# A gated recurrence followed by a highway layer: loads in runs of 4 KB, a product transposed by plain matmuls, and three products in two PSUM slots

## The chip, the cores and the metric

The kernel runs on one core of a Trainium2 chip. The metric is the device time of one execution in microseconds; lower is better. Times of a kernel are given as the median of its runs, with the lowest and highest.

## What is computed

The input has 4 sequences of 6336 tokens with 256 channels. First a gated linear recurrence runs along each sequence, for every channel on its own; then a highway layer with two 256 x 256 weights is applied to every token of the result. Cut to what matters:

```python
sig = 1.0 / (1.0 + np.exp(-f_logit))
f = lower_bound + (1.0 - lower_bound) * sig
i = 1.0 - f
for t in range(S):
    h = f[:, t] * h + i[:, t] * x[:, t]
    y[:, t] = h
...
H = np.maximum(y @ w_h, 0.0)
T = 1.0 / (1.0 + np.exp(-(y @ w_t + b_t)))
out = T * H + (1.0 - T) * y
```

Inputs and output are float32. x, f_logit and the output have 26 MB each, so about 78 MB cross the memory interface.

## The kernel before

**Tiling.** The tokens are cut into 29 units of work. Two small ones hold the first 192 tokens of two sequences each, on 96 partitions. The rest goes in steps of 1024 tokens, sequence by sequence, so that the four recurrences are carried side by side: a unit has 8 blocks of 128 tokens. The first such unit is split in two of 512 tokens, the last in 512, 256 and 256. There are 22 full units. The 256 channels are handled as two halves of 128.

**One unit, step by step.**

- `load` (L76) brings `lt` (from f_logit) and `xt` (from x) into SBUF, tokens on partitions. A partition gets one token of each block, so each run in memory is one token, 1 KB. Loads and stores are issued on SP's queue, four units ahead.
- `gate` (L140), on ACT, makes `u = sigmoid(-lt)` in float16. `product` (L152), on GpSimd (POOL), makes `bv = u * xt` in bfloat16.
- `decay_pe` (L178) and `b_pe` (L192) transpose `u` and `bv` on TensorE (PE) into PSUM (`uT`, `bT`), with channels on partitions and time along the row. Each transposes blocks of 128 x 128, eight for a half unit.
- `decay_act` (L185), on ACT, makes the decay `f = 1 + (lb - 1) u` from `uT`.
- `scan` (L201), on VectorE (DVE), runs the recurrence over `f` and `bT` into `y`; a half unit is one instruction of 1024 steps.
- `g_pe` and `z_pe` (both through `ffn_pe`, L212) multiply `y` by the weights, into PSUM tiles `gp` and `zp`.
- `t_act` (L227), on ACT, makes `t = sigmoid(z + b)` from `zp`. `d_dve` (L233), on DVE, makes `d` from `gp` and `y`; `e_dve` (L242) makes `e = d * t`, three quarters on DVE and one quarter on GpSimd.
- `o_pe` (L257) brings `y` and `e` back to tokens on partitions, with 16 matmuls for each half of four blocks, into PSUM tile `op`; the stationary operand takes every fourth column, so that a partition holds four tokens that follow each other. `o_act` (L271) copies `op` to SBUF on ACT and stores it in runs of 4 KB.

For units of 512 tokens and fewer, `both` (L164) puts the two channel halves into one PSUM tile.

**Order.** The order on each engine is written out by hand in the loop from L282 and pinned, so that PE, DVE, ACT and POOL take their instructions in just that order. With `n` the unit that is scanned, `p = n - 1` and `pp = n - 2`, one turn of the loop gives, for full units:

```
PE:  z(p,0)  o(pp,0)  uT(n+1,0)  bT(n,1)  z(p,1)  g(p,1)  o(pp,1)  bT(n+1,0)  uT(n+1,1)  g(n,0)
ACT: t(p,0)  o copy(pp,0)  f(n+1,0)  t(p,1)  u(n+2)  o copy(pp,1)  f(n+1,1)
DVE: scan(n,0)  d(p,0)  scan(n,1)  d(p,1)  e(p)
```

**PSUM.** A PSUM tile is taken from a pool by its tag, and a slot is given out again when the last reader of its former tile is done. The eight banks of 2 KB per partition are used thus, all from the pool `ps1` with one slot for each tag:

| tile | type, size per partition | slots |
|---|---|---|
| uT | float16, 2 KB | 1 |
| bT | bfloat16, 2 KB | 1 |
| gp | float32, 4 KB | 1 |
| zp | float32, 4 KB | 1 |
| op | float32, 4 KB | 1 |

Of the kernel before, what the change touches and what calls it, by code (L numbers as in the profile page):

```python
# [11 lines left out]
FP32 = mybir.dt.float32  # L12
BF16 = mybir.dt.bfloat16
FP16 = mybir.dt.float16
AF = mybir.ActivationFunctionType
# [4 lines left out]
def kernel(  # L20
# [16 lines left out]
    nc = tc.nc  # L37
    B, S, D = x.shape
    assert D == 256
    P = 128  # L40
    NH = D // P
    NB = 8
# [5 lines left out]
    units = []  # L48
# [4 lines left out]
    for s0 in range(rest, S, NB * P):  # L53
        for b in range(B):
            last = s0 + NB * P == S and b == B - 1
            a = s0
# [11 lines left out]
    outp = ctx.enter_context(tc.tile_pool(name="outp", bufs=4))  # L68
    ps1 = ctx.enter_context(tc.tile_pool(name="ps1", bufs=1, space=bass.MemoryType.PSUM))

    st = [dict() for _ in range(NU)]

    def pin(ins):
        return tc.keep_in_program_order(ins)

    def load(n, name, src):  # L76
        np_, nb, _, b, a = units[n]
        t = inp.tile([P, NB, D], FP32, tag=name, name=name)
        if isinstance(b, int):
            pin(nc.sync.dma_start(t[:, :nb], src[b, a:a + nb * P, :].rearrange("(j p) d -> p j d", p=P)))  # L80
        else:
            t4 = t[:np_, :nb].rearrange("p (b j) d -> p b j d", j=2)
            for j in range(2):
                pin(nc.sync.dma_start(t4[:, :, j], src[b, a + j * np_:a + (j + 1) * np_, :].rearrange("b p d -> p b d")))
        st[n][name] = t

    def store(n, j0, j1):
# [19 lines left out]
    for n in range(2):  # L107
        load(n, "lt", f_logit)
        load(n, "xt", x)

    ident_b = singles.tile([P, P], BF16, name="ident_b")
# [6 lines left out]
    ncc = singles.tile([P, NH], FP32, name="ncc")  # L118
# [42 lines left out]
    def width(n):  # L161
        return units[n][0] * units[n][1]

    def both(n, m, key, make):  # L164


        if width(n) > 512:
            st[n][key, m] = make()
            yield st[n][key, m], m, 0
        elif m == 0:  # L170
            st[n][key, 0] = st[n][key, 1] = t = make()
            for k in range(NH):
                yield t, k, k * 512

    def col(n, m):
        return 0 if width(n) > 512 else m * 512

    def decay_pe(n, m):  # L178
        np_, nb = units[n][:2]
        for uT, h, c in both(n, m, "uT", lambda: ps1.tile([P, NB * P], FP16, tag="uT", name="uT")):  # L180
            for j in range(nb):
                pin(nc.tensor.transpose(uT[:, c + j * np_:c + (j + 1) * np_], st[n]["u"][:np_, j, h * P:(h + 1) * P],  # L182
                                        ident_h[:np_, :np_]))

    def decay_act(n, h):  # L185
        N, c = width(n), col(n, h)
        if h == 0:
            st[n]["f"] = mid.tile([P, NH, NB * P], FP16, tag="f", name="f")
        pin(nc.scalar.activation(st[n]["f"][:, h, :N], st[n]["uT", h][:, c:c + N], AF.Identity,  # L189
                                 scale=ncc[:, h:h + 1], bias=1.0))  # L190

    def b_pe(n, m):  # L192
        np_, nb = units[n][:2]
        for bT, h, c in both(n, m, "bT", lambda: ps1.tile([P, NB * P], BF16, tag="bT", name="bT")):
            for j in range(nb):
                pin(nc.tensor.transpose(bT[:, c + j * np_:c + (j + 1) * np_], st[n]["bv"][:np_, j, h * P:(h + 1) * P],  # L196
                                        ident_b[:np_, :np_]))

    carry = {}

# [10 lines left out]

    def ffn_pe(n, m, key, k):  # L212
        N = width(n)
        for p, h, c in both(n, m, key, lambda: ps1.tile([P, NB * P], FP32, tag=key, name=key)):
            for ki in range(NH):
                for a in range(0, N, 512):
                    e = min(a + 512, N)
                    pin(nc.tensor.matmul(p[:, c + a:c + e], w_sb[:, k, ki, h * P:(h + 1) * P], st[n]["y"][:, ki, a:e],  # L218
                                         start=ki == 0, stop=ki == NH - 1))

    def g_pe(n, m):
        ffn_pe(n, m, "gp", 0)

    def z_pe(n, m):
        ffn_pe(n, m, "zp", 1)
# [29 lines left out]
    QB = NB // 2  # L255

    def o_pe(n, q):  # L257
        op = ps1.tile([P, QB, D], FP32, tag="op")
        np_, nb, _, b, _ = units[n]
        j0, j1 = q * QB, min((q + 1) * QB, nb)  # L260
        g = j1 - j0 if isinstance(b, int) else 2
        for j in range(j0, j1):
            k, i = divmod(j - j0, g)
            cols = slice((j0 + k * g) * np_ + i, (j0 + (k + 1) * g) * np_, g)
            for h in range(NH):
                o = op[:np_, j - j0, h * P:(h + 1) * P]
                pin(nc.tensor.matmul(o, st[n]["y"][:, h, cols], diag[:, h], start=True, stop=False))  # L267
                pin(nc.tensor.matmul(o, st[n]["e"][:, h, cols], ident_b, start=False, stop=True))  # L268
        st[n]["op"] = op
# [12 lines left out]
    for n in range(-3, NU + 2):  # L282
        if ok(n + 4) and n + 4 > 1:
            load(n + 4, "lt", f_logit)
            load(n + 4, "xt", x)
        p, pp = n - 1, n - 2
# [8 lines left out]
        if ok(pp):  # L295
            o_pe(pp, 0)
            o_act(pp, 0)
        if ok(n + 1):
            decay_pe(n + 1, 0)
            decay_act(n + 1, 0)  # L300
        if ok(p):
            d_dve(p, 0)
        if ok(n):
            b_pe(n, 1)
# [14 lines left out]
        if ok(pp) and units[pp][1] > QB:  # L319
            o_pe(pp, 1)  # L320
            o_act(pp, 1)
        if ok(n + 1):
            b_pe(n + 1, 0)
            decay_pe(n + 1, 1)
            decay_act(n + 1, 1)
# [38 lines left out]
```

## Time and profile before

Two runs took 228.53 and 225.68 us; the median is 227.11 us. The profiled execution has a span of 226.9 us from the first to the last instruction; the page gives no other time of its own for that execution.

| engine | busy us | share of the span |
|---|---|---|
| PE (matmul) | 195.0 | 86% |
| DVE | 202.1 | 89% |
| ACT | 199.1 | 88% |
| POOL | 140.0 | 62% |

The main groups on the engines, full units alone:

| line | operation | count | mean ns |
|---|---|---|---|
| L207 | DVE scan, 1024 steps | 44 | 2342 |
| L237 | DVE d, 1024 elements | 44 | 1256 |
| L249 | DVE e, 1536 elements | 22 | 958 |
| L143 | ACT u, 2048 elements | 22 | 1927 |
| L189 | ACT f, 1024 elements | 44 | 1136 |
| L231 | ACT t, 1024 elements | 44 | 1119 |
| L276 | ACT copy of o, 1024 elements | 47 | 1013 |
| L156 | POOL product, 512 elements | 96 | 1171 |

The DMA moved 78.69 MB in 60262 packets, 53584 of them under 2 KB, at a mean of 347 GB/s.

How to read it: busy time counts an engine from the start to the end of its instructions, and matmuls overlap each other in the records, so that PE's share says little about how close PE is to its limit; the distance between the starts of matmuls says more. A share over the whole span also mixes the start, the steady part and the tail. The steady part is read from a table by stage and from a timeline, and what counts there is the distance from one unit's scan to the next unit's. The row PEclk gives the clock that TensorE was granted, in tenths of full speed.

### The profile page before, as it was taken

The page shows a single profiled execution, that of the slowest core. Times are in us where ns is not written, and L with a number is a line of the kernel's source. Part 1 is how long each engine was busy: PE and PEld are TensorE (multiplying, and loading weights), DVE is VectorE, ACT ScalarE, POOL GpSimd, SP SyncE. Part 2 cuts the span into 40 slices and gives each one's busy share as a digit, 9 for nine tenths or more (in the row PEclk, how much of TensorE's full clock was granted, in tenths as well). Part 3 has the DMA queues.
Part 4 walks back from the last instruction along what each step waited for, and adds up shares of the span by engine and source line. Part 5 has one row for each costly group of instructions (what it writes and reads, how often), then busy time and mean ns, then how long its engine had stood idle before and what let it go on. Part 6 is the DMA issues. An engine that isn't in the chain of part 4 may idle for free.

```text
span 226.9 us, 4999 instructions
## 1 busy us (share of the span) xinstructions
PE 195.0 (86%) x2008; PEld 136.9 (60%) x2008; DVE 202.1 (89%) x159; ACT 199.1 (88%) x198; POOL 140.0 (62%) x131
## 2 busy tenths in 40 slices
PE   0588495989999999999999999999999999998971
PEld 0356365656766666676666657666665766665661
DVE  1499657799999999999999999999999999999871
ACT  4459946799999999999999999999999999976873
POOL 2654870745966786696678669667866966764300
PEclk9999857899999999999999999999999999999998
DMA  6999999999999999999999999999999997542444
GB/s 179 307 386 386 383 390 390 390 390 387 399 385 385 399 394 389 384 397 382 382 391 395 388 390 402 395 384 403 396 387 397 396 349 276 202 185 95 185 185 185
DMA packets 60262, 78.69 MB, mean 347 GB/s; under 512 B 2384, under 2 KB 53584, under 8 KB 60240
## 3 DMA queue, kind: packets, MB, share of 16 engines
q1 hardware_dynamic: 59152, 77.86, 93.9%
q10 hardware_dynamic: 1088, 0.53, 0.9%
q8 instruction: 15, 0.25, 0.4%
q14 instruction: 7, 0.06, 0.1%
HBM read 52.43 MB, written 25.95 MB: 345 GB/s over the span
## 4 chain that ended last, share of the span: by engine, by line
DVE 52%; issue 23%; PE 13%; DMA 4%; ACT 3%; POOL 3%; DVEq 0%; SPq 0%; ACTq 0%; POOLq 0%
DVE y L207 25%; DVE d L237 19%; DVE e L249 8%; PE gp L218 4%; PE zp L218 3%; POOL bv L156 3%; DMA xt<-in_x_dram 2%; PE bT L196 2%; PE uT L182 2%; DMA lt<-in_f_logit_dram 1%; PE op L267 1%; PE op L268 1%; ACT o L276 1%; ACT u L143 1%; ACT t L231 1%
## 5 line engine op out<-in xcount | busy, mean ns | idle before, releaser
L156 POOL TENSOR_TENSOR bv<-u,xt 128x512 bf16<-128x512 f16 (+1 forms) x100 | 114.3, 1172 | 18.9 <-DMA xt<-in_x_dram 7.2
L207 DVE TENSOR_TENSOR_SCAN y<-f,y,bT 128x1024 bf16<-128x1024 f16 (+2 forms) x54 | 113.7, 2105 | 7.9 <-PE bT L196 7.6
L231 ACT ACTIVATE t<-zp,bt 128x1024 bf16<-128x1024 f32 (+3 forms) x58 | 56.9, 994 | 13.5 <-PE zp L218 13.5
L218 PEld LDWEIGHTS <-w_sb 128*128 128x128 f16 x408 | 39.7, 100 | 43.1 <-issue 10.0
L237 DVE SCALAR_TENSOR_TENSOR d<-y,ncc,gp 128x1024 bf16<-128x1024 bf16 (+3 forms) x58 | 63.8, 1101 | 1.0 <-PE gp L218 0.9
L189 ACT ACTIVATE f<-uT,ncc 128x1024 f16<-128x1024 f16 (+3 forms) x58 | 58.4, 1007 | 4.2 <-PE uT L182 4.2
L251 POOL TENSOR_TENSOR e<-d,t 128x512 bf16<-128x512 bf16 x22 | 25.5, 1159 | 56.3 <-PE gp L218 56.3
L218 PE MATMUL gp<-y,w_sb 128*128 128x512 bf16 (+2 forms) x204 | 53.3, 385 | 3.7 <-DVE d L237 1.3
L218 PE MATMUL zp<-y,w_sb 128*128 128x512 bf16 (+2 forms) x204 | 52.6, 382 | 0.1
L267 PE MATMUL op<-diag,y 128*128 128x128 f16 (+1 forms) x400 | 50.8, 221 | 2.2 <-ACT o L276 2.2
L276 ACT COPY o<-op 128x1024 f32<-128x1024 f32 (+2 forms) x51 | 50.9, 997 | 1.9 <-PE op L268 1.7
L143 ACT ACTIVATE u<-lt 128x2048 f16<-128x2048 f32 (+3 forms) x29 | 49.0, 1689 | 3.9 <-DMA lt<-in_f_logit_dram 3.9
L268 PE MATMUL op<-ident_b,e 128*128 128x128 bf16 (+1 forms) x400 | 50.8, 220 | 0.0
L268 PEld LDWEIGHTS <-e 128*128 128x128 bf16 (+1 forms) x400 | 44.9, 115 | 7.5 <-POOL bv L156 1.3
L267 PEld LDWEIGHTS <-y 128*128 128x128 bf16 (+1 forms) x400 | 45.0, 114 | 5.7 <-issue 0.3
L196 PE MATMUL bT<-ident_b,bv 128*128 128x128 bf16 (+1 forms) x400 | 32.8, 224 | 16.6 <-DVE y L207 8.3
L196 PEld LDWEIGHTS <-bv 128*128 128x128 bf16 (+1 forms) x400 | 26.9, 100 | 23.8 <-issue 15.2
L182 PE MATMUL uT<-ident_h,u 128*128 128x128 f16 (+1 forms) x400 | 32.4, 227 | 5.7 <-ACT u L143 5.7
L182 PEld LDWEIGHTS <-u 128*128 128x128 f16 (+1 forms) x400 | 26.1, 103 | 6.1 <-ACT u L143 5.7
L249 DVE TENSOR_TENSOR e<-d,t 128x1536 bf16<-128x1536 bf16 (+3 forms) x29 | 25.9, 892 | 3.6 <-ACT t L231 0.8
L207 DVE TENSOR_TENSOR_SCAN y<-f,bT 128x192 bf16<-128x192 f16 x8 | 3.9, 536 | 4.1 <-PE bT L196 4.1
L117 DVE TENSOR_SCALAR cc<-lb 128x2 f32<-128x2 f32 x1 | 0.2, 169 | 3.8 <-DMA lb<-in_lower_bound_dram 3.8
(16 smaller groups left out, 6.8 us busy)
## 6 DMA issues: line engine op xcount, KB each, us to landing
out_dram<-o SPq DMA_DIRECT2D x47, 512.0 KB, 7.2
lt<-in_f_logit_dram SPq DMA_DIRECT2D x22, 1024.0 KB, 9.4
xt<-in_x_dram SPq DMA_DIRECT2D x22, 1024.0 KB, 11.3
lt<-in_f_logit_dram SPq DMA_DIRECT2D x3, 512.0 KB, 7.6
xt<-in_x_dram SPq DMA_DIRECT2D x3, 512.0 KB, 6.7
lt<-in_f_logit_dram SPq DMA_DIRECT2D x4, 192.0 KB, 3.7
xt<-in_x_dram SPq DMA_DIRECT2D x4, 192.0 KB, 3.9
out_dram<-o SPq DMA_DIRECT2D x2, 384.0 KB, 9.3
```

Of the source, the lines that this page charges most:

```text
L143: pin(nc.scalar.activation(u[:np_, :nb], st[n]["lt"][:np_, :nb], AF.Sigmoid, scale=-1.0))
L156: ins = pin(nc.gpsimd.tensor_mul(bv[:np_, q:q + 2], st[n]["u"][:np_, q:q + 2], st[n]["xt"][:np_, q:q + 2]))
L182: pin(nc.tensor.transpose(uT[:, c + j * np_:c + (j + 1) * np_], st[n]["u"][:np_, j, h * P:(h + 1) * P], ident_h[:np_, :np_]))
L189: pin(nc.scalar.activation(st[n]["f"][:, h, :N], st[n]["uT", h][:, c:c + N], AF.Identity, scale=ncc[:, h:h + 1], bias=1.0))
L196: pin(nc.tensor.transpose(bT[:, c + j * np_:c + (j + 1) * np_], st[n]["bv"][:np_, j, h * P:(h + 1) * P], ident_b[:np_, :np_]))
L207: pin(nc.vector.tensor_tensor_scan(y[:, h, c0:c0 + ln], st[n]["f"][:, h, c0:c0 + ln], st[n]["bT", h][:, col(n, h) + c0:col(n, h) + c0 + ln ...
L218: pin(nc.tensor.matmul(p[:, c + a:c + e], w_sb[:, k, ki, h * P:(h + 1) * P], st[n]["y"][:, ki, a:e], start=ki == 0, stop=ki == NH - 1))
L231: pin(nc.scalar.activation(st[n]["t"][:, m, :N], st[n]["zp", m][:, c:c + N], AF.Sigmoid, bias=bt[:, m:m + 1]))
L237: pin(nc.vector.scalar_tensor_tensor(st[n]["d"][:, m, :N], st[n]["y"][:, m, :N], ncc[:, m:m + 1], st[n]["gp", m][:, c:c + N], op0=ALU.mult ...
L267: pin(nc.tensor.matmul(o, st[n]["y"][:, h, cols], diag[:, h], start=True, stop=False))
L268: pin(nc.tensor.matmul(o, st[n]["e"][:, h, cols], ident_b, start=False, stop=True))
L276: pin(nc.scalar.copy(st[n]["o"][:np_, j0:j1], st[n]["op"][:np_, :j1 - j0]))
```

## The change

Three things are changed together.

1. **Loads.** A partition now gets four tokens that follow each other (for the small first units and the units of 256 tokens two), so that a run is 4 KB (or 2 KB). The first two units' loads are one transfer each in place of two. Blocks therefore hold every fourth token, and the columns have to be brought into time order on the way to the scan.
2. **Time order.** For `f`, ACT reads `uT` at a step and writes in time order. For `bT`, PE writes at a step: the transposes become plain matmuls with the identity, whose output is float32 at a step of four words (two for the small units). `bT` so grows from 2 KB to 4 KB per partition.
3. **PSUM.** `uT` moves to a pool with two slots. `gp`, `zp` and `op` share one tag, `zg`, with two slots of 4 KB. The sum is again eight banks: 4 KB for `bT`, 2 x 4 KB for `zg`, 2 x 2 KB for `uT`.

`o_pe` computes its columns with the same step as before (four, and two for the small units). The loop and its order on each engine are not touched.

```diff
+    ps2 = ctx.enter_context(tc.tile_pool(name="ps2", bufs=2, space=bass.MemoryType.PSUM))
+
+    ps3 = ctx.enter_context(tc.tile_pool(name="ps3", bufs=2, space=bass.MemoryType.PSUM))
...
         if isinstance(b, int):
-            pin(nc.sync.dma_start(t[:, :nb], src[b, a:a + nb * P, :].rearrange("(j p) d -> p j d", p=P)))
+            g = min(nb, 4)
+            pin(nc.sync.dma_start(t[:, :nb].rearrange("p (s j) d -> p s j d", j=g),
+                                  src[b, a:a + nb * P, :].rearrange("(s p j) d -> p s j d", p=P, j=g)))
         else:
-            t4 = t[:np_, :nb].rearrange("p (b j) d -> p b j d", j=2)
-            for j in range(2):
-                pin(nc.sync.dma_start(t4[:, :, j], src[b, a + j * np_:a + (j + 1) * np_, :].rearrange("b p d -> p b d")))
+            pin(nc.sync.dma_start(t[:np_, :nb].rearrange("p (b j) d -> p b j d", j=2),
+                                  src[b, a:a + 2 * np_, :].rearrange("b (p j) d -> p b j d", j=2)))
...
-        for uT, h, c in both(n, m, "uT", lambda: ps1.tile([P, NB * P], FP16, tag="uT", name="uT")):
+        for uT, h, c in both(n, m, "uT", lambda: ps3.tile([P, NB * P], FP16, tag="uT", name="uT")):
...
-        pin(nc.scalar.activation(st[n]["f"][:, h, :N], st[n]["uT", h][:, c:c + N], AF.Identity,
-                                 scale=ncc[:, h:h + 1], bias=1.0))
+        nb, b = units[n][1], units[n][3]
+        g = min(nb, 4) if isinstance(b, int) else 2
+        pin(nc.scalar.activation(
+            st[n]["f"][:, h, :N].rearrange("c (s p j) -> c s p j", s=nb // g, j=g),
+            st[n]["uT", h][:, c:c + N].rearrange("c (s j p) -> c s p j", s=nb // g, j=g), AF.Identity,
+            scale=ncc[:, h:h + 1], bias=1.0))
...
-        for bT, h, c in both(n, m, "bT", lambda: ps1.tile([P, NB * P], BF16, tag="bT", name="bT")):
+        g = min(nb, 4) if isinstance(units[n][3], int) else 2
+        for bT, h, c in both(n, m, "bT", lambda: ps1.tile([P, NB * P], FP32, tag="bT", name="bT")):
             for j in range(nb):
-                pin(nc.tensor.transpose(bT[:, c + j * np_:c + (j + 1) * np_], st[n]["bv"][:np_, j, h * P:(h + 1) * P],
-                                        ident_b[:np_, :np_]))
+                k, i = divmod(j, g)
+                at = c + k * g * np_
+                pin(nc.tensor.matmul(bT[:, at + i:at + g * np_:g], st[n]["bv"][:np_, j, h * P:(h + 1) * P],
+                                     ident_b[:np_, :np_], start=True, stop=True))
...
-        for p, h, c in both(n, m, key, lambda: ps1.tile([P, NB * P], FP32, tag=key, name=key)):
+        for p, h, c in both(n, m, key, lambda: ps2.tile([P, NB * P], FP32, tag="zg", name=key)):
...
-        op = ps1.tile([P, QB, D], FP32, tag="op")
+        op = ps2.tile([P, QB, D], FP32, tag="zg")
         np_, nb, _, b, _ = units[n]
         j0, j1 = q * QB, min((q + 1) * QB, nb)
-        g = j1 - j0 if isinstance(b, int) else 2
+        g = min(nb, 4) if isinstance(b, int) else 2
         for j in range(j0, j1):
-            k, i = divmod(j - j0, g)
-            cols = slice((j0 + k * g) * np_ + i, (j0 + (k + 1) * g) * np_, g)
+            k, i = divmod(j, g)
+            cols = slice(k * g * np_ + i, (k + 1) * g * np_, g)
```

## The prediction

> **What bounds the kernel now.** First the page's busy table and its slices.
>
> ```profile
> PE 195.0 (86%) x2008; PEld 136.9 (60%) x2008; DVE 202.1 (89%) x159; ACT 199.1 (88%) x198; POOL 140.0 (62%) x131
> ...
> DVE  1499657799999999999999999999999999999871
> ...
> PEclk9999857899999999999999999999999999999998
> DMA  6999999999999999999999999999999997542444
> ```
>
> Three engines and the DMA all look full, so the shares decide nothing. The table by stage separates them:
>
> ```profile
> 30.00:35.00 5.00, 5.00 (x38) 3.31 (x37) 1.74 (x2) 2.43 (x4) 3.09 (x3) 0.60 1.08 390
> ...
> 60.00:100.00 40.00, 37.93 (x403) 26.61 (x402) 39.48 (x26) 39.17 (x37) 28.63 (x26) 1.00 1.07 390
> 215.00:220.00 5.00, 3.55 (x51) 3.08 (x48) 3.70 (x7) 4.20 (x9) 0.77 (x1) 1.00 0.37 150
> ```
>
> (columns after the stretch: PE, PEld, DVE, ACT, POOL busy, then clock, DMA share, GB/s). From 60 to 100 us DVE works 39.48 of 40 us, ACT 39.17. The timeline of one iteration there shows the order inside it:
>
> ```profile
> 119.65 1.03 PE L218 MATMUL zp<-y,w_sb 128*128 128x512 bf16 x4
> 119.71 2.34 DVE L207 TENSOR_TENSOR_SCAN y<-f,y,bT 128x1024 bf16<-128x1024 f16 x1
> 120.77 1.11 ACT L231 ACTIVATE t<-zp,bt 128x1024 bf16<-128x1024 f32 x1 [0.16 <-PE zp L218]
> 121.78 1.00 ACT L276 COPY o<-op 128x1024 f32<-128x1024 f32 x1
> 121.97 1.25 DVE L237 SCALAR_TENSOR_TENSOR d<-y,ncc,gp 128x1024 bf16<-128x1024 bf16 x1
> 122.11 0.61 PE L196 MATMUL bT<-ident_b,bv 128*128 128x128 bf16 x8
> 123.14 2.34 DVE L207 TENSOR_TENSOR_SCAN y<-f,y,bT 128x1024 bf16<-128x1024 f16 x1
> ```
>
> The first scan starts at 111.79 and again at 119.71: the period is **7.92 us**, and DVE fills it: scan to d 2.26, d to scan 1.17, scan to d 2.26, d to e 1.36, e to the next scan 0.87, in all 7.92. ACT follows with starts 0.89 (o to f), 1.01 (f to t), 0.99 (t to u), 1.81 (u to o), 0.89, then a 0.2 us pause for z, 1.01: it has about 0.25 us to spare per unit. PE issues four z/g groups at 0.86, two o groups at 0.89, four transposing groups at 0.43: 6.94 us, and spends the other 0.98 in three short waits on DVE. DMA moves 3.15 MB per unit, 7.9 to 8.1 us at 390 to 397 GB/s. So DVE sets the pace and every other engine has little slack. About 20 such iterations run from 48 to 206 us.
>
> **Part 1: the loads in longer runs.** It takes nothing out of DVE's 7.92 us; the transfers already keep pace. It can pay only before 48 us, where products wait on xt 7.2 us in all, in three waits. The first two units' loads go from eight issues to four; on SP's queue a pair takes 0.88 to 1.03 us and a single one about 0.40, so up to 2 us of issue goes. The chain then leaves the transfers (ACT at 20.48 us). Bounds: 0 and 2.5 us gained; I take 1.5. [...]
>
> **Part 2: f reads uT at a step.** Same 1024 elements. ACT's price is per element whatever the type: (1136 - 700)/512 = 0.85 ns for f16 and (1119 - 694)/512 = 0.83 for f32. No ACT row reads at a step; the nearest stepped operand is the weight load of y, 114 ns against 100 for contiguous bv. Bounds: 0 and 14%, 0.16 us per f. I take 0 and leave the other end to the range; two uT slots hide nothing, since uT waits for no slot in the steady part now.
>
> **Part 3: bT by plain matmuls, float32 at a step of four words.** The count stays 8 per half. The scan costs 2.08 ns per element ((2342 - 1275)/512) against 1.04 ns for d, which reads float32 PSUM ((1256 - 726)/512); its own recurrence limits it, so I let it stay at 2.34. The matmul's price is unknown: no row writes at a step. Lower end: contiguous float32 output, op L268, one per 55 ns. Upper end: the row where each column takes about two cycles, the op matmuls near 33 us at clock 0.60, one per 107 ns. Eight cost 0.43 or 0.86 us. The two ends are close, and I take the middle. [...]
>
> **Part 4: two slots for g, z and o.** This is the part that decides. Today each of the three has its own slot. When PE comes to the o of the first half, right behind z(p,0), one slot holds z(p,0) until t(p,0) has read it, the other holds g(p,0) until d(p,0) has. Now t ends at 121.88 and d at 123.22, so z's slot is free first, and o takes it. PE, in order, stands from the end of z's issue (0.86) until t is done (1.12 + 1.11 = 2.23): about 1.4 us. Behind it on PE stand uT, bT for the second scan, z and g of the second half; ACT, which copied o right behind t, has nothing to do; DVE's second scan waits for bT. Today this is hidden by op's own slot.
>
> The new loop, by starts, with z(p,0) at 0: t at 1.12 (111.73 to 112.85), ends 2.23; o on PE at 2.28 (0.05 from ACT's end to PE, as at 216.5 us); 16 matmuls take 1.06 and 0.09 to ACT, so the copy starts at 3.43; f 4.32; t(p,1) 5.33; u 6.32; second copy 8.13, ends 9.15; its slot is what the next z takes: **9.20**. The other way round, on PE: t(p,1) ends 6.45, second o needs that slot: 6.50 + 0.89 + bT 0.43 + uT 0.44 + g 0.86 = 9.12. So both agree at 9.2 with 55 ns. With 107 ns: uT ends issuing at 3.61, bT 4.47, t(p,1) 5.59, its end 6.70, then 6.75 + 0.89 + 0.86 + 0.44 + 0.86 = 9.80. Middle 9.50. DVE needs 7.92 and now waits.
>
> **The sum**, on the profiled span of 226.9: 20 x (9.50 - 7.92) = +31.6. Before 48 us the same wait falls on the chain three times (o behind t at 18.7, 32.8 and 42.1 us) at 1.3: +3.9, less 1.5 of Part 1: +2.4. The case around 24 us is covered by the 4.97 us of products there. In the tail four iterations have it, at most 4.8; ACT idles 4.7 us there, so I take half: +2.4. Together 263.3; the page gives no other time of its own for that execution, and the median of the two runs is 227.11, 0.2 above the span: **263.5**. The forecast's own range is 252 (9.2 and nothing at the ends) to 273 (9.8 and 7 us at the ends).
>
> **Rivals.** (a) *The o takes g's slot and waits for d(p,0)*, should the pool hand the slots out in that order. Then DVE is in the loop: 0.06 + o 0.89 + uT 0.44 + bT 0.61 + 0.09 + 2.26 + 1.36 + 0.87 + 2.26 + 1.25 = 10.1, or 10.5 at 107 ns: +43.6 to +51.6, with the ends 275 to 283. For it: only the times of today's schedule say that t is first. Against it: t leads by 1.34 us. (b) *The step costs more than twice*: 214 ns, a quarter rate, adds 0.86 twice to 9.80: 11.5, near 303; f at 14% more adds 3 us to any case. For it: no row bounds it from above. Against it: the step on the weight load costs only 14%. (c) *PE's clock falls* because PE now stands still: at 30 us it ran at 0.60 after a stretch with 2.70 of 5 us busy. At half rate PE's 6.94 becomes 13.9: +120 us. Against it: at 215 us 3.55 of 5 kept clock 1.00, and the new loop has 6.9 to 7.8 of 9.2 to 9.8. (d) *Not slower*: the transfers, at a share of 0.99, are the true pacemaker, and longer runs release the loop. At the tail's rate, 185 GB/s at a share of 0.44, some 420 GB/s, a unit is 7.5 us: 20 x 0.42 = 8.4 off, near 218. It decides only if ACT and PE can swallow the 1.2 us wait, that is if o's wait is below ACT's 0.25 us of slack; DVE's 39.48 of 40 and its gap-free starts speak against it. If only the wait is swallowed and DVE still leads, it gives about 226.
>
> **How the numbers follow.** Forecast 0.65; (a) 0.14; (b) 0.10; (c) 0.03; (d) 0.08, half of it under -2% and half within. Two per cent is about what a measurement of this kernel can tell from no change (its two runs lie 1.3% apart). So faster 0.04, same 0.04, slower 0.92. The range 252 to 286 holds the forecast, (a) and the low part of (b); left out are (c), (d) and most of (b).
>
> **What would show it.** In the changed profile: idle time of PE at L267 ended by ACT t L231, about 1.4 us in each iteration, and of ACT at L276 ended by PE op L268, about 1.2; scans 9.2 to 9.8 us apart; DVE down from 98.7% to about 83% of the steady part, with its idle time before L207; scan, d and e unchanged in length; bT matmuls 55 to 107 ns apart. The steps are wrong if L267 waits for DVE d instead (rival a), if eight bT matmuls take over 1 us (b), if the clock row falls under 9 (c), or if scans stay 7.9 us apart (d).

## The result, and the profile after

The changed kernel takes 293.5 us (293.28 to 293.71, two runs) against 227.11 us (225.68 to 228.53) before: a ratio of 1.292, with a 95% interval of 1.272 to 1.311. The forecast was slower, at 263.5 us with a range of 252 to 286; the time lies above the range. The profiled execution took 293.28 us at a span of 291.5, so a time is about 1.8 us more than its span. The profiled execution of the kernel before (span 226.9 us, mean granted clock 0.974) is one of its slower ones: in the runs beside the experiments, those at a clock of 0.973 to 0.981 had spans of 226.3 to 227.4 us and the others 222.3 to 225.8.

The page's table and slices of the changed kernel, as shown for the kernel before:

```profile
PE 215.6 (74%) x2008; PEld 157.5 (54%) x2008; DVE 204.0 (70%) x159; ACT 204.3 (70%) x198; POOL 139.5 (48%) x131
...
DVE  1287756984876786695696696697676687678761
...
PEclk9999799997999999997999999999997999999999
DMA  7999997939589779778589778877976742513243
```

DVE does the same work as before (204.0 against 202.1 us) in a span that is 65 us longer, and no engine is full any more: the engines wait for each other in a loop. The line of one period, from a table by stretches (PE, PEld, DVE, ACT, POOL busy, then clock, DMA share, GB/s), says the same of the steady part:

```profile
156.52:167.06 10.54, 8.19 (x82) 6.01 (x81) 7.91 (x5) 7.97 (x8) 5.65 (x5) 1.00 0.85 317
```

DVE works 7.91 of **10.54 us**; the period was 7.92. The timeline of such a period:

```profile
151.01 1.03 PE L230 MATMUL zp<-y,w_sb 128*128 128x512 bf16 x4
152.13 1.11 ACT L243 ACTIVATE t<-zp,bt 128x1024 bf16<-128x1024 f32 x1 [0.53 <-PE zp L230]
152.73 1.25 DVE L249 SCALAR_TENSOR_TENSOR d<-y,ncc,gp 128x1024 bf16<-128x1024 bf16 x1
154.04 0.22 PE L279 MATMUL op<-diag,y 128*128 128x128 f16 x1 [2.00 <-DVE d L249]
...
154.93 0.61 PE L187 MATMUL uT<-ident_h,u 128*128 128x128 f16 x8
155.13 1.01 ACT L288 COPY o<-op 128x1024 f32<-128x1024 f32 x1 [1.88 <-PE op L280]
155.37 1.04 PE L208 MATMUL bT<-ident_b,bv 128*128 128x128 bf16 x8
...
156.21 1.07 PE L230 MATMUL zp<-y,w_sb 128*128 128x512 bf16 x4
156.52 2.35 DVE L219 TENSOR_TENSOR_SCAN y<-f,y,bT 128x1024 bf16<-128x1024 f16 x1 [2.53 <-PE bT L208]
```

A bracket gives the idle time before an instruction and what ended it. PE stands 2.00 us ahead of the first o, until **d** has ended (152.73 + 1.25 = 153.98; the o starts at 154.04). t had ended at 153.24, 0.74 us earlier. Behind the o come uT and bT, and the second scan has waited 2.53 us when bT is there. That is the place that the forecast named, with the other releaser: rival (a). The waits over the whole span (engine and line, what they waited for, then us in all, times, longest) add up to the same picture; in the last line it is mostly the o of the second half that waits for t:

```profile
DVE y L219 <- PE bT L208: 67.0, 26, 5.1
...
ACT o L288 <- PE op L280: 45.9, 31, 1.9
PE op L279 <- DVE d L249: 41.9, 23, 2.0
...
PE op L279 <- ACT t L243: 13.5, 26, 2.2
```

The groups by shape show what single instructions cost now:

```profile
L219 DVE TENSOR_TENSOR_SCAN y<-f,y,bT 128x1024 bf16<-128x1024 f16 x44 | 103.2, 2345 | 59.7 <-PE bT L208 59.7
...
L208 PE MATMUL bT<-ident_b,bv 128*128 128x128 bf16 x384 | 53.5, 324 | 3.3 <-DVE y L219 3.3
...
L196 ACT ACTIVATE f<-uT,ncc 128x1024 f16<-128x1024 f16 x44 | 49.4, 1122 | 2.0 <-PE uT L187 2.0
```

Scan (2342 before) and f (1136 before) kept their price; a bT matmul went from 222 to 324 ns, and in the timeline eight of them take 156.21 - 155.37 = 0.84 us, 104 ns each, where the transposes took 55.

Where the 64.6 us of span went, by the start of the first scan of the seventh unit (from which on the period was steady before) and of the last full unit, 19 periods later:

| us of span | before | after | difference |
|---|---|---|---|
| up to the seventh unit | 48.4 | 54.5 | +6.1 |
| 19 periods | 150.5 | 202.5 | +52.0 |
| from the last full unit on | 28.0 | 34.5 | +6.5 |

The 48.4 holds a stretch at a low clock (0.72, 0.60 and 0.74 in the three stretches from 25 to 40 us). Experiments 10 to 12 below have the kernel before's time, the same 150.5 us of 19 periods and the same 28.0 us at the end, and there the seventh unit begins at 45.4 to 46.0 us. So the first line's loss is 6.1 us against this profile and some 8.5 to 9.1 us against such a start (an estimate from those three runs).

### The profile page after: what moved, and what is told of

Read it like the earlier page. It is cut to its first block, busy times and chain, and to the rows that moved or that the text cites. A ratio compares the mean times of both kernels' runs of the same rounds, so it can differ in the third digit from the quotient of the medians.

```text
span 291.5 us, 4989 instructions
## 1 busy us (share of the span) xinstructions
PE 215.6 (74%) x2008; PEld 157.5 (54%) x2008; DVE 204.0 (70%) x159; ACT 204.3 (70%) x198; POOL 139.5 (48%) x131
## 4 chain that ended last, share of the span: by engine, by line
DVE 49%; PE 28%; issue 12%; DMA 5%; ACT 4%; DVEq 0%; ACTq 0%
DVE y L219 23%; DVE d L249 19%; PE bT L208 9%; DVE e L261 7%; PE op L279 6%; PE uT L187 5%; PE op L280 4%; DMA w_raw<-in_moe_w_h_dram 3%; PE zp L230 3%; PE gp L230 2%; ACT t L243 2%; DMA lt<-in_f_logit_dram 1%; ACT u L148 1%; ACT f L196 1%; ACT o L288 1%
## 5 line engine op out<-in xcount | busy, mean ns | idle before, releaser
L279 PE MATMUL op<-diag,y 128*128 128x128 f16 (+1 forms) x400 | 50.4, 219 | 55.4 <-DVE d L249 41.9
L230 PEld LDWEIGHTS <-w_sb 128*128 128x128 f16 x408 | 41.5, 106 | 40.9 <-issue 5.0
L208 PE MATMUL bT<-ident_b,bv 128*128 128x128 bf16 (+1 forms) x400 | 56.6, 328 | 7.5 <-DVE y L219 4.8
L196 ACT ACTIVATE f<-uT,ncc 128x1024 f16<-128x1024 f16 (+3 forms) x58 | 57.7, 995 | 4.0 <-PE uT L187 4.0
L230 PE MATMUL zp<-y,w_sb 128*128 128x512 bf16 (+2 forms) x204 | 54.9, 394 | 1.1 <-ACT o L288 1.1
L230 PE MATMUL gp<-y,w_sb 128*128 128x512 bf16 (+2 forms) x204 | 52.0, 378 | 2.4 <-DVE w_sb L141 2.4
L208 PEld LDWEIGHTS <-bv 128*128 128x128 bf16 (+1 forms) x400 | 43.5, 137 | 9.2 <-POOL bv L161 5.4
L279 PEld LDWEIGHTS <-y 128*128 128x128 bf16 (+1 forms) x400 | 44.8, 114 | 5.5
L187 PE MATMUL uT<-ident_h,u 128*128 128x128 f16 (+1 forms) x400 | 33.6, 230 | 5.7 <-ACT u L148 5.7
L187 PEld LDWEIGHTS <-u 128*128 128x128 f16 (+1 forms) x400 | 28.5, 108 | 6.1 <-ACT u L148 5.7
```

The source lines that it names most:

```text
L196: pin(nc.scalar.activation(st[n]["f"][:, h, :N].rearrange("c (s p j) -> c s p j", s=nb // g, j=g), st[n]["uT", h][:, c:c + N].rearrange("c ...
L208: pin(nc.tensor.matmul(bT[:, at + i:at + g * np_:g], st[n]["bv"][:np_, j, h * P:(h + 1) * P], ident_b[:np_, :np_], start=True, stop=True))
```

## The experiments

Theory S: the order in which the two slots are given out makes the loop. Its rival W: PE has too much work with the stepped writes, whatever the slots.

**1. The slots alone, in the kernel before.**

```diff
+    ps2 = ctx.enter_context(tc.tile_pool(name="ps2", bufs=2, space=bass.MemoryType.PSUM))
...
-        for p, h, c in both(n, m, key, lambda: ps1.tile([P, NB * P], FP32, tag=key, name=key)):
+        for p, h, c in both(n, m, key, lambda: ps2.tile([P, NB * P], FP32, tag="zg", name=key)):
...
-        op = ps1.tile([P, QB, D], FP32, tag="op")
+        op = ps2.tile([P, QB, D], FP32, tag="zg")
```

> The kernel before with the one edit that g, z and o share two slots; loads, transposes and bT as before. Theory S: o of the first half waits for d(p,0); period 0.06 + 0.89 + 0.44 + 0.61 + 0.09 + 2.26 + 1.36 + 0.87 + 2.26 + 1.25 = 10.1 us, span 226.9 + 20 x 2.17 + about 6 at the ends = 276 us. Rival W (the slots cost little, the stepped writes are the loss): period under 8.5 us, span under 240 us.

It took 282.33 us, span 280.2, in one run (226.19 us before, median of seven runs on that chip). Its period, from the timeline of DVE:

```profile
128.75 2.35 DVE L208 TENSOR_TENSOR_SCAN y<-f,y,bT 128x1024 bf16<-128x1024 f16 x1 [2.11 <-PE bT L197]
...
138.87 2.35 DVE L208 TENSOR_TENSOR_SCAN y<-f,y,bT 128x1024 bf16<-128x1024 f16 x1 [2.11 <-PE bT L197]
```

138.87 - 128.75 = 10.12 us, 10.1 expected. The slots alone make most of the loss: +3.1 us up to the seventh unit, +44.1 in the 19 periods, +6.1 at the end. The span is 4 us over the expected one: the ends took 9.2 us in place of 6, and three of the periods took 11.2 to 11.7 us while one took only 8.4.

**2. All but the slots.** bT is cut to 2 KB per partition, so that g, z and o can have a slot each again within the 16 KB that the tiles took before.

```diff
-                pin(nc.tensor.matmul(bT[:, at + i:at + g * np_:g], st[n]["bv"][:np_, j, h * P:(h + 1) * P],
+                at0 = k * g * np_ if np_ * nb <= 512 else 0
+                pin(nc.tensor.matmul(bT[:, at0 + i:at0 + g * np_:g], st[n]["bv"][:np_, j, h * P:(h + 1) * P],
...
-                y[:, h, c0:c0 + ln], st[n]["f"][:, h, c0:c0 + ln], st[n]["bT", h][:, col(n, h) + c0:col(n, h) + c0 + ln],
+                y[:, h, c0:c0 + ln], st[n]["f"][:, h, c0:c0 + ln],
+                st[n]["bT", h][:, min(c0 + ln, 512) - 1:min(c0 + ln, 512)].to_broadcast([P, ln]),
...
-        op = ps2.tile([P, QB, D], FP32, tag="zg")
+        op = ps1.tile([P, QB, D], FP32, tag="op")
```

> The changed kernel with a slot of its own for each of g, z and o as before, one slot for uT, and bT kept to one bank: the second four blocks of the product are written over the first, and each scan takes one column of bT for all its steps, so the recurrence's input is left out; number and kind of instructions, 4 KB loads, stepped reads of uT and stepped writes of bT are those of the changed kernel. Theory S: without the shared slots PE has 6.94 + 2 x 0.43 = 7.8 us of work in a unit and DVE leads again, period 7.9 to 8.1 us, span 229 to 236 us with the later start. Rival W: PE cannot hold 7.92 us, period 9 us or more, span over 250 us.

It took 233.11 us, a ratio of 1.028 to the kernel before (1.018 to 1.038). The timeline of DVE:

```profile
131.22 2.34 DVE L215 TENSOR_TENSOR_SCAN y<-f,y,bT 128x1024 bf16<-128x1024 f16 x1
133.48 1.25 DVE L246 SCALAR_TENSOR_TENSOR d<-y,ncc,gp 128x1024 bf16<-128x1024 bf16 x1
134.76 2.35 DVE L215 TENSOR_TENSOR_SCAN y<-f,y,bT 128x1024 bf16<-128x1024 f16 x1
...
139.26 2.34 DVE L215 TENSOR_TENSOR_SCAN y<-f,y,bT 128x1024 bf16<-128x1024 f16 x1
```

The period is 8.03 us. The stepped writes cost nearly nothing where they lie beside DVE's work: d to scan takes 1.28 in place of 1.17. The eight stepped matmuls between the two scans begin at 133.62 and last 1.03 us, to 134.65, and the second scan starts at 134.76: they end a little later than d covers. Over 19 periods that is 2.1 us; the rest of the 2.8% lies at the start, where experiment 8 finds a loss from the loads. Rival W has fallen.

**3. The slots by hand: z and o share one, g has its own.** So the o can wait for t alone, as in the forecast's loop.

```diff
-        for p, h, c in both(n, m, key, lambda: ps2.tile([P, NB * P], FP32, tag="zg", name=key)):
+        for p, h, c in both(n, m, key, lambda: ps2.tile([P, NB * P], FP32, tag="g" if key == "gp" else "zo", name=key)):
...
-        op = ps2.tile([P, QB, D], FP32, tag="zg")
+        op = ps2.tile([P, QB, D], FP32, tag="zo")
```

(the pool `ps2` then has one slot for each tag.)

> The changed kernel with its two 4 KB slots given out by hand: g has one of its own, z and o share the other, so that o of the first half takes z's slot and waits for t, not for d. Theory S (the order in which the slots went is what failed in the forecast): the wait at the first o ends with t(p,0), DVE leaves the loop, the period falls from 10.54 to about 9.8 us and the time from 291.5 to about 277 us of span. Rival W (the stepped writes, 107 ns each, make PE the bound whatever the slots): the period stays at 10.5 and the span at 290 us or more.

It took 279.55 us, span 277.8, in one run.

```profile
133.71 1.11 ACT L243 ACTIVATE t<-zp,bt 128x1024 bf16<-128x1024 f32 x1 [0.53 <-PE zp L230]
134.31 1.25 DVE L249 SCALAR_TENSOR_TENSOR d<-y,ncc,gp 128x1024 bf16<-128x1024 bf16 x1
134.88 0.22 PE L279 MATMUL op<-diag,y 128*128 128x128 f16 x1 [1.26 <-ACT t L243]
...
137.36 2.35 DVE L219 TENSOR_TENSOR_SCAN y<-f,y,bT 128x1024 bf16<-128x1024 f16 x1 [1.79 <-PE bT L208]
```

The o now waits for t and starts while d still runs; the period is 9.80 us in nearly all units, the forecast's value at 107 ns. The choice of the slot is worth 10.54 - 9.80 = 0.74 us per unit. The span is 13.7 us shorter: 16.5 us in the 19 periods, less 3.2 us at the end, where this run takes 37.6 us from the last full unit on. So even the loop that the forecast had in mind runs to 277.8 us.

**4. The same slots in the kernel before**, with its transposes and loads: the forecast's loop at 55 ns.

> The kernel before with one edit: z and o share one slot of 4 KB, g keeps its own; loads and transposes as before. This is the forecast's loop without the stepped writes: period 9.20 us by its working, from 48 to 206 us 20 x 1.28 = 26 us more, some 12 us more at the ends as in the run with z and o in one slot, span about 264 us. Rival: the loop has another limit than o waiting for t, period over 9.5 us.

It took 269.26 us, span 267.1, in one run; the period is 9.37, not 9.20.

```profile
130.09 0.22 PE L267 MATMUL op<-diag,y 128*128 128x128 f16 x1 [1.26 <-ACT t L231]
...
132.25 1.02 PE L218 MATMUL zp<-y,w_sb 128*128 128x512 bf16 x4 [0.21 <-ACT o L276]
```

The working of 9.20 lacks one wait that this arrangement has: with one slot for z and o, the z of the second half waits for the copy of o (0.21 us here). In experiment 3 the copy ends at 136.98 us and the z, behind the longer bT, starts at 137.04, so the same wait costs nothing there. That 9.80 was met so closely is in part luck.

**5. The product written contiguously.**

```diff
-                pin(nc.tensor.matmul(bT[:, at + i:at + g * np_:g], st[n]["bv"][:np_, j, h * P:(h + 1) * P],
+                pin(nc.tensor.matmul(bT[:, c + j * np_:c + (j + 1) * np_], st[n]["bv"][:np_, j, h * P:(h + 1) * P],
```

> The changed kernel with the product written contiguously (plain matmuls, float32, step 1), so the product's time order is left out. Theory S: each of the eight bT matmuls falls from about 104 to 55 ns, 0.43 us less in the loop, period 10.1, span about 282 us. Rival W: with the steps gone most of the loss goes, span under 250 us.

It took 283.17 us, span 281.4, in one run; the period is 10.12. So inside the loop the step costs 0.42 us per unit, about 8 us over 19 periods.

**6 and 7. What in the step costs.** Two other patterns of the same output: pairs of neighbouring words at a step of eight words, and single words at a step of two. They tell a price on every gap (rival Q) and a price that grows with the step (rival R) from a price on words that stand alone.

```diff
-                pin(nc.tensor.matmul(bT[:, at + i:at + g * np_:g], st[n]["bv"][:np_, j, h * P:(h + 1) * P],
+                pin(nc.tensor.matmul(bT[:, at:at + g * np_].rearrange("c (m i t) -> c m i t", i=g, t=2)[:, :, i], st[n]["bv"][:np_, j, h * P:(h + 1) * P],
```

```diff
+                pin(nc.tensor.matmul(bT[:, at + i // 2 * 2 * np_ + i % 2:at + (i // 2 + 1) * 2 * np_:2], st[n]["bv"][:np_, j, h * P:(h + 1) * P],
```

> The changed kernel with each bT matmul writing two neighbouring words, then a gap (pairs at a step of eight words) instead of single words at a step of four; the product's time order is left out. [...] Rival Q (any gap in the output costs): 104 ns each, period 10.5, span about 291 us.

> The changed kernel with a step of two words instead of four in the bT matmuls' output; the product's time order is left out. [...] Rival R (the price grows with the step): between 55 and 104 ns, period 10.2 to 10.4, span 284 to 288 us.

The pairs took 282.62 us (span 280.8, period 10.12), the step of two 293.79 us (span 292.0, period 10.54), one run each. The bT matmuls (ns: least, median, most), of the pairs first, of the step of two second:

```profile
L208 PE MATMUL bT<-ident_b,bv x400: 216/219/314, 8.0 to 269.8; 128*128 128x128 bf16 x128, 96*128 96x96 bf16 x6
```

```profile
L208 PE MATMUL bT<-ident_b,bv x400: 269/314/502, 7.9 to 281.1; 128*128 128x128 bf16 x128, 96*128 96x96 bf16 x6
```

Pairs cost what a contiguous output costs (217/220/315 in experiment 5); a single word costs the same at a step of two as at four, where the changed kernel's line reads 269/314/502. Rivals Q and R fall: in these runs the words that stand alone cost; why, no run shows. All pairs here began at an even word; pairs that begin at an odd one were not run.

**8 to 12. The late start.** In the changed kernel the weights are used from 15.20 us on, in place of 10.80. All five runs below are the kernel before with longer load runs and no other edit of the change.

> The kernel before with the longer load runs alone; the time order is not restored, so each unit is scanned in another order of its tokens. Theory L (the weights' 1 KB packets on ACT's queue come late among 4 KB packets on SP's): weights at about 15 instead of 10.8 us, steady period 7.92 as before, unit 6 begins its first scan at about 51 instead of 48.4 us, span 229 to 230 us. Rival G (the forecast's Part 1): the longer runs bring the start forward by 1.5 us, span about 225 us.

Measured: 230.71 us, ratio 1.0196 (1.011 to 1.028). The 19 periods take 150.5 us, as before; the weights are used from 14.66 us on. The forecast's gain isn't there.

```diff
+        if n == 0:
+            for k, w in enumerate((moe_w_t, moe_w_h)):
+                pin(nc.sync.dma_start(w_raw[:, 1 - k], w.rearrange("(h p) o -> p h o", p=P)))
...
-        for k, w in enumerate((moe_w_t, moe_w_h)):
-            pin(nc.scalar.dma_start(w_raw[:, 1 - k], w.rearrange("(h p) o -> p h o", p=P)))
```

> As the run with the longer load runs alone (time order not restored), with the two weight transfers put on SP's own queue right behind the first unit's loads instead of on ACT's queue. Theory L: the weights are there before 10 us, the late start goes, unit 6 begins by about 48 us and the span is 225 to 227 us. Rival: the start is late because the first units' own transfers are late, not the weights; moving 0.5 MB ahead of the second unit's loads costs another 1.3 us, span 230 to 231 us.

Measured: 229.79 us, ratio 1.014 (1.007 to 1.022). The weights are used from 12.11 us on without a wait, but the second unit's lt now comes at 9.6 us in place of 7.9. The interval overlaps the one above: inconclusive.

> The kernel before with longer load runs in all units but the first two, which load as before (time order not restored). Theory F (the start is late because the first two units' own transfers land later: products began at 7.4 instead of 5.9 us): the start is as before, ratio 1.00. Theory L (the weights wait among the 4 KB packets of the units behind): weights still at 13 to 15 us, ratio 1.01 to 1.02.

Measured: ratio 1.000 (0.995 to 1.005), weights used from 11.19 us on. The ratio is the one of theory F, and L in that form falls: the loads of the later units had runs of 4 KB here too. The loss comes with the first two units' loads; by which of their properties, this run doesn't say.

> The kernel before with longer load runs in the full units alone; the small units and the split ones load as before (time order not restored). Theories F and L: nothing with long runs is in flight before some 10 us, weights at about 11 us, ratio 1.00 (0.995 to 1.005). Rival U (the long runs of the full units do it themselves, by filling all buffers at a higher rate at the cost of something else): ratio 1.015 or more.

Measured: ratio 1.0005 (0.997 to 1.004). Rival U falls.

What is it in the first two units, the longer run or the smaller number of issues? The last run keeps the run of 2 KB and gives back the number (against the loads of the changed kernel):

```diff
-            pin(nc.sync.dma_start(t[:np_, :nb].rearrange("p (b j) d -> p b j d", j=2),
-                                  src[b, a:a + 2 * np_, :].rearrange("b (p j) d -> p b j d", j=2)))
+            for k in range(2):
+                pin(nc.sync.dma_start(t[:np_, 2 * k:2 * k + 2],
+                                      src[b.start + k, a:a + 2 * np_, :].rearrange("(p j) d -> p j d", j=2)))
```

> The kernel before with the longer load runs alone (time order not restored), but each load of the first two units issued as two transfers again, one for each sequence, with runs of 2 KB: eight issues as before, where the run with the longer loads alone had four. Theory I (with four issues the queue is free 1 us sooner, and the third unit's loads, 1 MB, start beside the weights): with eight issues the weights are there at about 11 us and the ratio is 1.00. Rival J (the 2 KB runs on 96 partitions themselves are late): ratio 1.02 as with the longer loads alone.

Measured: ratio 0.997 (0.994 to 1.001). The issues on SP's queue, with four loads for the first two units:

```profile
2.15 0.45 SPq L84 DMA_DIRECT2D xt<-in_x_dram  x1
5.02 0.35 SPq L81 DMA_DIRECT2D lt<-in_f_logit_dram  x1
5.42 0.43 SPq L81 DMA_DIRECT2D xt<-in_x_dram  x1
6.55 0.33 SPq L81 DMA_DIRECT2D lt<-in_f_logit_dram  x1
7.93 0.33 SPq L81 DMA_DIRECT2D xt<-in_x_dram  x1
```

and with eight:

```profile
3.61 0.98 SPq L85 DMA_DIRECT2D xt<-in_x_dram  x2
5.44 0.35 SPq L81 DMA_DIRECT2D lt<-in_f_logit_dram  x1
6.77 0.35 SPq L81 DMA_DIRECT2D xt<-in_x_dram  x1
7.36 0.45 SPq L81 DMA_DIRECT2D lt<-in_f_logit_dram  x1
9.73 0.33 SPq L81 DMA_DIRECT2D xt<-in_x_dram  x1
```

With four issues the third unit's xt goes out at 5.42 in place of 6.77 and the fourth unit's at 7.93 in place of 9.73, beside the weights that ACT's queue issues at 4.9 and 5.3 us; these land 6.6 and 9.3 us after their issue, against 5.3 and 6.6 with eight. That the number of issues decides (four of 384 KB or eight of 192 KB, with the same runs of 2 KB) is shown: ratios of 1.0196 and 0.997. That the weights share the transfers with loads that nobody needs yet is the reading that fits; it was not tried by itself.

## Why the prediction was wrong, and where it was right

**The step that failed is the choice of the slot in Part 4.** The forecast let the o take z's slot, because t ended 1.34 us ahead of d in the timeline of before. In the changed kernel the o takes g's slot in the full units, although t is ready first there too (by 0.74 us in the period shown). Which slot a tile gets is settled when the program is put together, not on the chip. In the built program the tiles of the full units lie in the two slots strictly in turn, in the order of the loop: z(p,0), o(pp,0), z(p,1), g(p,1), o(pp,1), g(n,0). Each tile so takes the place of the one two before it: o(pp,0) that of g(p,0), read by d, and o(pp,1) that of z(p,1), read by t. These are the two waits of L279 above, for d 23 times and for t 26 times. Only the o's of the first three units lie where z was, so the turn is no rule to rely on; why the slots were given out so stays open. A timeline of the kernel before could not tell it, and (a), with its chance of 0.14, should have weighed at least as much as the forecast's choice. The choice costs 0.74 us in each period, 14.1 us in 19. With the slot that the forecast chose, the time is 279.55 us (experiment 3): 16 above 263.5, but within 252 to 286.

**Part 3 was mis-sized**: 104 ns per matmul, near the upper end, where the middle, 81, was taken: 9.80 in place of 9.50, 5.7 us in 19 periods. The 107 ns of the upper end were read at a granted clock of 0.50 (32 to 34 us of the kernel before), the 104 at 1.00 (146.52 to 157.06 us of the changed kernel). That scan and d keep their price was right, and so was f in Part 2. The trace of before has no matmul that writes at a step, so the middle was the author's estimate. In the timeline of the changed kernel the single words cost about twice what contiguous ones do, 104 ns (bT) against 55 (op); pairs cost no more than a contiguous output, 224 against 228 ns on average in the groups by shape of experiments 6 and 5.

**Part 1 had the wrong sign**: 1.5 us gained was forecast, 4.4 us were lost (0.0196 x 226.35). The issues saved were counted as time won; by the reading that fits, they moved the following loads in beside the weights. The text priced what the queue saves and not what the earlier loads get in the way of. The transfers did become faster, though, as the table by stretches of the kernel before and of the longer loads alone shows (last two columns: DMA share, GB/s):

```profile
15.00:20.00 5.00, 4.84 (x50) 3.94 (x48) 4.63 (x7) 4.37 (x8) 2.60 (x3) 1.00 1.09 386
```

```profile
15.00:20.00 5.00, 3.97 (x21) 2.45 (x22) 4.59 (x11) 1.11 (x3) 0.31 (x1) 1.00 1.02 420
```

By these two rows the longer runs move 9% more in the same time. On its own that gained no time: in experiments 10 to 12 the ratios are 1.000, 1.0005 and 0.997, and DVE led, busy for 39.37 and 39.48 of the 40 us from 100 to 140 us in experiments 10 and 11.

**The ends**: up to the seventh unit +2.4 was forecast and +6.1 came (experiment 1, the slots alone, has 3.1; experiment 2, all but the slots, 2.5, or some 5 against a start at 45.4 to 46.0 us); from the last full unit on +2.4 and +6.5 (slots 6.1). Halving the tail for ACT's idle time was wrong: in the chain of the changed kernel from 250 us on, d, o, uT, bT and scan follow each other, DVE and PE in turn, and ACT has only 5% of it (o 3.8%, t 1.2%), so each wait counts in full. And the time was set 0.2 us above the span, where it lies 1.8 above.

**The sum.** The span is 291.5 where the forecast's was 263.3, 28.2 us more. The slot makes 14.1, Part 3 5.7, the ends 7.8 (12.6 in place of 4.8) and the three long periods, less a short one, 2.2; 1.6 go off again, since the forecast counted 20 periods and the table 19.

**What was right**: that DVE led before and that a shared slot puts a wait in its place, the wait's place and who stands behind it, the arithmetic of both loops (9.80 and 10.5 worked out, 9.80 and 10.54 measured), and that the transfers bounded nothing (their share in the steady part is 1.07 by the forecast's own rows; the 0.99 of rival (d) is the row from 180 to 190 us). Rival (a) at 107 ns has the right mechanism; its 283 had the ends too small. Rival (c) came in small: three of the 19 periods took 11.6 to 11.8 us, with the clock row at 7 in their slices. Rivals (b) beyond a factor of two and (d) fell. The upper end of the forecast's own range, 273, is a slip: its terms give 226.9 + 20 x 1.88 + 7 + 0.2 = 271.7.

No run gives a version faster than the kernel before. Longer load runs were worth nothing while DVE set the pace (ratios of 1.000, 1.0005 and 0.997 in experiments 10 to 12), and with a slot of their own for g, z and o a float32 bT brings the tiles to 18 KB per partition, 4 x 4 KB and 2 KB for uT, where those of both kernels take 16; no run has that. Own slots together with the old start were not run.

## What to carry to other kernels

When tiles with different readers come to share slots, read from the built program which slot each tile gets, or give the slots out by hand with a tag for each. Where that can't be done, work out one loop for each slot that the waiting instruction can get, and carry all of them at full weight; a schedule of before doesn't settle it. The step in the output of these matmuls was priced by whether neighbouring words came in pairs (219 ns in the records) or stood alone (314), and it cost next to nothing (0.11 us per unit in experiment 2) where the writes lay beside the leading engine's work. Saving DMA issues moved the later transfers forward (the third unit's xt went out at 5.42 us in place of 6.77): look which other transfers they then run beside before counting it as a gain.

## What the runs showed of the hardware that was not expected

- The bT matmuls of 128 columns, with float32 output, took 219 ns in the records (median) when words came in pairs and 314 when each word stood alone, at a step of two (experiment 7) as at four (the changed kernel). The contiguous o matmuls, 219 ns in the records too, start 55 ns apart in the changed kernel's timeline; the bT matmuls at a step of four start 104 ns apart. At a lowered clock it was about twice that: from 69.03 to 70.66 us of the changed kernel, at a granted clock of 0.50, eight stepped matmuls took 1.63 us, 204 ns each.
- Loads in 4 KB runs (the longer loads alone, experiment 8) moved 420 GB/s where the 1 KB runs of the kernel before moved 386, in the stretch from 15 to 20 us, with the DMA share at 1.02 and 1.09.
- ACT's f read PSUM at a step of 128 float16 elements at no higher price: 1122 ns in the changed kernel against 1136 before.
